# One more seven-product group for tile pairs 8 and 9, other planner costs, and a last product cut at column 256 in a fused attention and feed-forward kernel

## The chip, the cores and the metric

The kernel runs on one core of one Trainium2 chip. The metric is the device time of one execution in microseconds (us). A core has TensorE (PE in the profile; its weight loads are listed apart as PEld), VectorE (DVE), ScalarE (ACT), GpSimd (POOL), which here mostly issues loads, and SyncE (SP), which here issues stores. Each engine takes its instructions in the order in which they were written; engines wait for each other by semaphores.

## The reference

Softmax attention over 8 batches of 12 heads (448 tokens, head size 64) is followed by a feed-forward block over all 3584 tokens. Inputs and output are float32.

```python
def _attn_ref(q, k, v):
    scores = (1.0 / np.sqrt(q.shape[-1])) * np.matmul(q, k.transpose(0, 1, 3, 2))
    scores = scores - np.max(scores, axis=-1, keepdims=True)
    attn = np.exp(scores)
    attn = attn / (np.sum(attn, axis=-1, keepdims=True) + 1e-09)
    return np.matmul(attn, v)

def _moe_ref(x, w_in, w_out):          # w_in 768x2048, w_out 2048x768
    h = x @ w_in
    g = h * (1.0 / (1.0 + np.exp(-h)))
    return g @ w_out

# x = attention's output, heads side by side: 3584 x 768
```

## The kernel before

The matrices are kept in float16, sums in float32 in PSUM. Attention runs batch by batch, interleaved with the feed-forward products of batches that are done. The last four batches go through the first product, x @ w_in, two at a time (`queue_pair`, batches 4 and 5, then 6 and 7), by Winograd's form of Strassen's method: seven products in place of eight, paid for with additions on DVE. The tiles named f are theirs.

The second product, g @ w_out, is made for pairs of 128-token tiles, numbered `qd` from 0 to 13, again by seven products (`queue_quad`, `product`). Product m of a pair is eight matmuls, each with 128x128 weights (a slice of g or of a sum of such slices) and 384 columns of w_out (or of a difference of its quarters). The sums of g, called S_5, S_6, S_3 and 7, come from `combine_g` (line 918), each in two DVE instructions of 128x512. Products gather in PSUM tiles named p; ACT copies four of them into output tiles (`take_copy`, line 1006), DVE adds the rest (`take_sum`, line 1025) and SP stores them: four issues of 32 rows for each block of 128x384, except for the last batch. Output tiles are called ost (four buffers, taken in turn) or wide (for pairs 8, 10 and 11).

Some products of two neighbouring pairs use the same right-hand matrix. `FOLD` on line 255 lists those that are joined: the first two numbers are the pairs, the last tuple the products. Two such products, 16 matmuls of 384 columns, then form one 2x2 block product, which is made once more by seven products of a quarter of its size: four matmuls of 192 columns each (`queue_fold`, `fold_product`). Its left-hand sums are four DVE instructions of 128x512 (`fold_x`, line 1084, tiles named fold); its right-hand sums are made once for each m (`fold_w`, line 1062, tiles named right and T), for m = 4 and m = 2. The results gather in two PSUM tiles, n_P and n_Q, which five DVE instructions add to the two output blocks (`fold_read`, lines 1123, 1126 and 1135). From the third entry of `FOLD` on (`MID`) a group runs among the products of its second pair, has its PSUM tiles from the common banks, and holds some of the attention's old buffers for its left-hand sums: three of the four rq buffers and one of the two rk buffers for m = 2.

The order of all instructions is made by a planner inside the kernel. `Order.step` advances a model of the engines: each `Op` has an engine, a duration in us, the ops that it needs and a bias that ranks it among those that are ready. PE takes the first product in the queue `moe` that is ready by this model (`moe_ready`). For DVE and ACT a part of each duration counts as overlap with the next instruction (`OVERLAP`, 0.07 us on DVE). What comes out is a fixed order for each engine; the durations in the `Op` calls are not times of the chip, they only decide that order.

The last product of all is product 2 of pair 13. It is made in two pieces, each with its own PSUM tile (p and p_2r), its own DVE addition and its own stores (`take_end`, line 1012): the first piece is stored by SP alone, 128 rows, the second by SP and ACT, 64 rows each.

```python
FOLD = ((10, 11, (2, 4)), (12, 13, (4,)), *((7, 8, (4,)),))
...
for c in range(2):
    for f0 in range(0, HF, 1):
        queue(2, f0, f0 + 1, OH // 2 * c, OH // 2 * (c + 1))
```

Of the kernel before, what the change touches and what calls it, by code (L numbers as in the profile page):

```python
# [29 lines left out]
def mm(n):  # L30
    return n / 2400.0 + 0.0026
# [183 lines left out]
def kernel(  # L215
# [25 lines left out]
    OH = DM // 2  # L241
# [10 lines left out]
    FAR = (NT * B // 4 - 1,)  # L252
    BROAD = NT * B // 4 - 3
    WIDE = (NT * B // 4 - 6, NT * B // 4 - 4)
    FOLD = ((10, 11, (2, 4)), (12, 13, (4,)), *((7, 8, (4,)),))
    MID = 2
    AHEAD_OF = ((1, 4),)
    LEAD = 0
    TAIL = None
    folded = {(q, m) for a, b, ms in FOLD for q in (a, b) for m in ms}  # L260
    TWB, SXB = 40, 4
# [802 lines left out]
    def fold_x(g, m, i, at):  # L1064
        a, b = FOLD[g][:2]
        tag, n = at
# [19 lines left out]
    def fold_product(g, m, k):  # L1086
        a, b = FOLD[g][:2]
        x, y, bank, at, new = {
# [20 lines left out]
    def fold_read(g, m, k):  # L1109
        a, b = FOLD[g][:2]  # L1110
        i, j = {2: SUM[2], 4: OUT[4]}[m]
# [35 lines left out]
    od = Order(SHY)  # L1147
# [111 lines left out]
    def take_bank(name):  # L1259
        bank_of[name] = m_ring.take()  # L1260
# [357 lines left out]
    def plan_sums():  # L1618

        if not quads:  # L1620
            return
        qd, todo = quads[0]
        if len(todo) == 4:
            gates = {}
            for f in range(NFF):
                gates[f] = gates_at(2 * qd, f) + gates_at(2 * qd + 1, f)
                if None in gates[f]:
                    return
            gates_of[qd] = gates
        gates = gates_of[qd]  # L1630
        while todo and (todo[0] == 7 or sg_ring.can(1, od.now)):
            m = todo.pop(0)
            if m != 7:
                sg_ring.take()
            sg_op[(qd, m)] = []
            for f0 in (0, 4):
                deps = [x for f in range(f0, f0 + 4) for x in gates[f] + gates[f + HF]]
                if m != 5:
                    deps += sg_op[(qd, {6: 5, 7: 5, 3: 6}[m])]
                sg_op[(qd, m)].append(  # L1640
                    od.add(
                        Op(
                            "DVE",
                            0.40,
                            lambda m=m, f0=f0: combine_g(qd, m, f0, f0 + 4),
                            deps,
                            0,
                            then=lambda at, m=m: sum_read(qd, {6: 5, 3: 6}.get(m), at),
                        )
                    )  # L1650
                )
        if not todo:
            quads.pop(0)
# [3 lines left out]
    def plan_folds():  # L1657

        last = PAIRS[1]
        if "w" not in w2_op and last_pair and e_ring.can(1, od.now):  # L1660
            w2_op["w"] = True
            e_slot["spare"] = e_ring.take()
            for m in (4, 2):
                for i in (1, 2, 3, 4):
                    more = [w2_op[(m, i // 2)]] if i in (2, 4) else []
                    w2_op[(m, i)] = od.add(
                        Op("DVE", 0.57, lambda m=m, i=i: fold_w(m, i), last_pair + more, 1)
                    )
        if not folds or "w" not in w2_op:
            return  # L1670
        g, m, done = folds[0]
        made = [x for q in FOLD[g][:2] for f in range(HF, NFF) for x in gates_at(2 * q + m // 4, f)]
        n = len(x2_op) // 4
        if g < MID:
            if (last, HF - 1) not in pair_done:
                return
            made += [pair_done[(last, HF - 1)].get((i, j)) for i in range(2) for j in range(2)]
            if n > 2:
                made += [fold_done[n - 2].get(k) for k in (7, 2)]
        if None in made:  # L1680
            return
        held = ((rq_ring, 3), (rk_ring, 1)) if m == 2 else ((kt_ring, 2),)
        if g >= MID:
            if not all(r.can(k, od.now) for r, k in held):
                return
            for r, k in held:
                r.take(k)
            done["held"] = held
        folds.pop(0)
        homes = [("KT", 3)] * 3 + [("rk", NRK)] if n % 2 else [("rq", NRQ)] * 4  # L1690
        if g >= MID:
            homes = [("KT", 3)] * 2 + [("xT", NX3)] * 2 if m == 4 else [("rq", NRQ)] * 3 + [("rk", NRK)]
        for i in (1, 2, 3, 4):
            more = [x2_op[(g, m, i // 2)]] if i in (2, 4) else []
            x2_op[(g, m, i)] = od.add(
                Op("DVE", 0.43, lambda i=i: fold_x(g, m, i, homes[i - 1]), made + more, 1)
            )

    kept = []
# [96 lines left out]
    def queue_quad(qd):  # L1796
        quads.append((qd, [5, 6, 7, 3]))
        took = {}
# [14 lines left out]
        def queue(m, f0, f1, c0=0, c1=OH):  # L1813
            first = {6: (1,), 2: (1,), 7: (6, 5), 3: (5, 6) if qd == LAST else (5, 6, 7), 4: (7,)}.get(m, ())

            def run():
                strips = od.mode == "cols" and bool(qk_seq or av_seq)
                op = Op(
                    "PE",
                    (f1 - f0) * mm(c1 - c0),  # L1820
                    lambda: product(qd, m, f0, f1, strips, c0, c1),
                    tail=PE_OUT,
                )
                if BANK[m] == m and f0 == 0:
                    take_bank(f"p_{qd}_{m}" + "r" * (c0 > 0))
                for ring, need in rings:
                    ring.take(need)
                if m in (5, 6, 3) and f1 == HF:
                    op.then = lambda at: sum_read(qd, m, at)
                od.on_pe(op, "cols" if strips else "full", (f1 - f0) * (4 if strips else 1))  # L1830
                if f1 < HF or c1 < OH:
                    begun[m] = (HF if c0 else 0) + f1
                if f1 < HF:
                    return
                if c1 - c0 < OH:
                    fn = lambda: take_end(half_t[c0][:, 0 : c1 - c0], c0, c1)
                    od.add(Op("DVE", 0.33, fn, [op, took[1]], -4))
                    return
                pr_op[(qd, m)] = op
                read(m, [op] + [took[x] for x in {2: (1,), 7: (5,), 3: (6,)}.get(m, ())])  # L1840
                if m == 7 and (qd, 4) in folded:
                    if qd in ahead:
                        def then(at):
                            leave_bank(f"p_{qd}_1")(at)
                            home.give(at + STORE)

                        od.add(
                            Op(
                                "DVE",
                                OH / 960.0 + 0.13,  # L1850
                                lambda: take_last(qd),
                                [op, took[7], ahead[qd]],
                                -4,
                                then=then,
                            )
                        )
                    else:
                        read(4, [op, took[7]])

            def deps():  # L1860
                if f0 or c0:
                    return [] if begun.get(m) == (HF if c0 else 0) + f0 else [None]
                made = list(w_op.get(m, [None]))
                hard = {6: (1,), 7: (6,), 3: (5,), 4: (7,)}.get(m, ())
                made += [took.get(x) if x in hard else (took.get(x), 9.0) for x in first]
                if m in (1, 2, 4):
                    t = 2 * qd + m // 4
                    i = int(m != 1)
                    for f in range(HF):
                        made += [(y, f * mm(OH)) for y in gates_at(t, f + HF * i)]  # L1870
                    return made + ld_wout
                x = sg_op.get((qd, m), [None, None])
                return made + [x[0], (x[1], 4 * mm(OH))]

            rings = ((home, 1),) if f0 == 0 and (m in OUT or m == 7 and (qd, 4) in folded and qd not in ahead) else ()
            moe.append((deps, int(BANK[m] == m and f0 == 0), run, rings))


# [18 lines left out]
        if qd == LAST and TAIL:  # L1897
            ends.pop()()
        elif qd == LAST:
            for c in range(2):  # L1900
                for f0 in range(0, HF, 1):
                    queue(2, f0, f0 + 1, OH // 2 * c, OH // 2 * (c + 1))

    def after_x(n):

# [56 lines left out]
    qk_seq, av_seq = [], []  # L1962
# [287 lines left out]
    while True:  # L2250
# [45 lines left out]
        m = m_ring.when(1)  # L2296
# [43 lines left out]
```

## Time and profile before

| | us |
|---|---|
| median of 3 runs | 378.93 (378.29 to 379.14) |
| the profiled execution, device time | 378.17 |
| its span on the core | 376.4 |
| PE busy | 370.2 |
| DVE busy | 287.5 |
| ACT busy | 255.6 |

The span runs from the first to the last instruction of the core. Busy time is the time in which an engine had at least one instruction in work. A matmul in the records lasts longer than its distance to the next one, since matmuls are pipelined: 384 columns are shown with 326 ns and follow each other every 163, 192 columns are shown with 246 ns and follow every 82. DVE and ACT instructions overlap their neighbours in the records too, by some 0.08 and 0.1 us. In the timeline a line is one instruction, or several alike in a row ("x8"); the name before the arrow is what is written, the names behind it what is read, and a bracket tells how long the engine had been idle and what ended that.

### The profile page before, as it was taken

To read this page: it belongs to the slowest core of one execution; us is meant where nothing else is said; L and a number is where in the kernel's file an instruction comes from. 1 tells how busy PE (TensorE), PEld (TensorE's weight loads), DVE (VectorE), ACT (ScalarE), POOL (GpSimd) and SP (SyncE) were. 2 spreads that over 40 slices of the span, in tenths; PEclk is the share of its full clock that TensorE was granted. 3 is DMA by queue.
4 is the path that set the end of the run, shared out by engine and by line. 5 is a ranking of instruction groups with operands and counts; after the bars stand their busy time and mean duration, and the time that the engine had idled before them with its cause. 6 is when DMAs were issued, how large, how long until landed. Compare 5 with 4: busy or idle time off the path is not lost.

```text
span 376.4 us, 9978 instructions
## 1 busy us (share of the span) xinstructions
PE 370.2 (98%) x4030; PEld 188.0 (50%) x4030; DVE 287.5 (76%) x597; ACT 255.6 (68%) x401; POOL 85.0 (23%) x155
## 2 busy tenths in 40 slices
PE   7999999999999999999999999999999999999996
PEld 3365445444444444444444454545556655556764
DVE  3668858999995969995969998899379725449853
ACT  4988873896878787877788777658872238883130
POOL 6653337424016326006423200000000000000000
PEclk9999999999999999999999999999999999999999
DMA  7999999919049849147954411210002240001334
GB/s 113 198 208 209 207 200 181 205 21 132 16 96 153 154 51 123 27 94 108 176 91 67 57 46 44 55 32 0 0 3 53 74 108 20 0 1 34 84 96 126
DMA packets 35966, 34.47 MB, mean 92 GB/s; under 512 B 11856, under 2 KB 35152, under 8 KB 35920
## 3 DMA queue, kind: packets, MB, share of 16 engines
q0 software_dynamic: 25312, 22.82, 40.9%
q1 hardware_dynamic: 10064, 10.38, 10.1%
q10 hardware_dynamic: 544, 0.64, 0.5%
q8 instruction: 31, 0.51, 0.5%
q14 instruction: 15, 0.12, 0.1%
HBM read 45.61 MB, written 11.01 MB: 150 GB/s over the span
## 4 chain that ended last, share of the span: by engine, by line
PE 95%; ACT 3%; DMA 1%; DVE 0%; issue 0%; POOLq 0%
PE p L685 29%; PE h L685 21%; PE f L685 16%; PE s L448 11%; PE a L570 8%; PE o L685 3%; ACT E L504 2%; PE a L556 2%; PE a L603 2%; PE n_Q L685 1%; PE n_P L685 1%; DMA rk<-in_k_dram 1%; ACT T L493 1%; PE z L685 0%; PE p_2r L685 0%
## 5 line engine op out<-in xcount | busy, mean ns | idle before, releaser
L504 ACT ACTIVATE E<-s 128x896 f16<-128x896 f32 x164 | 141.9, 921 | 24.5 <-PE s L448 24.5
L685 PE MATMUL h<-xT,w_in_t 128*32 128x448 f16 (+2 forms) x762 | 83.5, 348 | 0.0
L685 PEld LDWEIGHTS <-w_in_t 128*128 128x128 f16 (+1 forms) x909 | 54.6, 97 | 50.0 <-issue 8.0
L354 POOL DMA_DIRECT2D V<-in_v_dram x88 | 48.5, 560 | 51.2 <-PE a L570 29.2
L685 PEld LDWEIGHTS <-G 128*128 128x128 f16 (+1 forms) x668 | 41.9, 97 | 28.0 <-issue 5.2
L717 ACT ACTIVATE th<-h 128x448 f16<-128x448 f32 x67 | 36.6, 546 | 24.2 <-PE h L685 20.7
L685 PE MATMUL p<-w_out_t,G 128*128 128x384 f16 (+2 forms) x326 | 51.8, 324 | 0.0
L448 PE MATMUL s<-rq,KT 32*128 32x448 f16 (+3 forms) x728 | 44.9, 347 | 1.4 <-DVE rq L412 0.9
L685 PEld LDWEIGHTS <-S 128*128 128x128 f16 (+1 forms) x321 | 29.5, 98 | 22.3 <-issue 3.4
L761 DVE SCALAR_TENSOR_TENSOR G<-th,h 128x448 f16<-128x448 f16 (+1 forms) x64 | 35.7, 573 | 4.8 <-ACT th L717 4.3
L685 PE MATMUL p<-D,S 128*128 128x384 f16 (+1 forms) x217 | 39.0, 326 | 0.0
L1006 ACT COPY ost<-p 128x384 f32<-128x384 f32 x38 | 18.2, 480 | 24.6 <-PE p L685 16.2
L570 PE MATMUL a<-E,V 128*32 128x448 f16 (+1 forms) x640 | 32.7, 356 | 0.0
L1025 DVE TENSOR_TENSOR ost<-p,ost 128x384 f32<-128x384 f32 x29 | 16.0, 553 | 18.4 <-ACT ost L1006 9.6
L673 DVE SCALAR_TENSOR_TENSOR xT<-a,rdn 128x448 f16<-128x448 f32 x46 | 27.0, 619 | 3.0 <-PE a L570 2.4
L334 POOL DMA_DIRECT2D rq<-in_q_dram x25 | 13.9, 559 | 67.3 <-PE s L448 57.9
L448 PEld LDWEIGHTS <-KT 32*128 32x128 f16 (+1 forms) x824 | 12.3, 96 | 31.5 <-issue 29.8
L517 DVE TENSOR_TENSOR T<-T,E 128x1792 f16<-128x1792 f16 x21 | 22.8, 1086 | 4.7 <-ACT E L504 4.7
L888 DVE TENSOR_TENSOR p<-f,p 128x448 f32<-128x448 f32 x15 | 9.4, 624 | 22.2 <-PE f L685 12.3
L517 DVE TENSOR_TENSOR T<-E,E 128x1792 f16<-128x1792 f16 x21 | 22.8, 1084 | 4.0 <-ACT E L504 4.0
L685 PE MATMUL f<-sx,tw 128*128 128x448 f16 x102 | 23.4, 352 | 0.0
L570 PEld LDWEIGHTS <-V 128*32 128x32 f16 (+1 forms) x640 | 13.5, 95 | 18.0 <-issue 10.1
(134 smaller groups left out, 464.5 us busy)
## 6 DMA issues: line engine op xcount, KB each, us to landing
out_dram<-ost SPq DMA_DIRECT2D x147, 48.0 KB, 1.8
rk<-in_k_dram POOLq DMA_DIRECT2D x24, 224.0 KB, 5.4
rq<-in_q_dram POOLq DMA_DIRECT2D x23, 224.0 KB, 5.7
w_out_t<-in_moe_w_out_dram POOLq DMA_DIRECT2D x4, 768.0 KB, 13.5
V<-in_v_dram POOLq DMA_DIRECT2D x42, 64.0 KB, 4.0
out_dram<-wide SPq DMA_DIRECT2D x48, 48.0 KB, 1.6
V<-in_v_dram POOLq DMA_DIRECT2D x42, 48.0 KB, 4.4
w_in_t<-in_moe_w_in_dram POOLq DMA_DIRECT2D x6, 256.0 KB, 8.7
```

Source lines behind the costliest of these rows:

```text
L334: nc.gpsimd.dma_start(out=rawq[n][:, cols], in_=group_of(q, b, hg)[:, cols])
L354: nc.gpsimd.dma_start(out=VT[b][32 * x : 32 * (x + 1), hs, at : at + count, :], in_=v[b, hs].rearrange("h (i g) d -> i h g d", g=TPP)[:, : ...
L448: nc.tensor.matmul(out=pS[p0 : p0 + 32 * (x1 - x0), h % 2, at : at + q1 - q0], lhsT=KT[(b, hg)][32 * h : 32 * (h + 1), key_rows(b, hg, c, ...
L504: nc.scalar.activation(out=E[(n, w)][:, 2 * y : 2 * y + 2, :], in_=pS_t[(n, w, y)][:, :, 0:S], func=AF.Exp, scale=attn_scale,)
L517: nc.vector.tensor_tensor(out=T[n], in0=T[n] if step else E[(n, 0)], in1=E[(n, step + 1)], op=ALU.add,)
L570: nc.tensor.matmul(out=a[32 * h : 32 * (h + 1), 0:S], lhsT=VT[b][k0:k1, HG * hg + h, place(b, hg, c), part - 1 :: 2], rhs=e[k0:k1, h], sta ...
L673: nc.vector.scalar_tensor_tensor(out=x3(b, cc)[:, cc % 3, 32 * g0 : 32 * g1], in0=acc[(n, part)][:, 0:nq], scalar=0.5, in1=rdn_t[n].rearra ...
L685: nc.tensor.matmul(out=out[i : i + cut], lhsT=w[:, i : i + cut], rhs=x, start=start, stop=stop, skip_group_check=True,)
L717: nc.scalar.activation(out=th, in_=h_t[(b, f, t0)][:, 0:n], func=AF.Tanh)
L761: nc.vector.scalar_tensor_tensor(out=dst[:, f, at + lo : at + hi], in0=th_t[(b, f, t0)][:, lo - t0 : hi - t0], scalar=1.0, in1=h_t[(b, f, ...
L1006: nc.scalar.copy(out=ost(qd, *OUT[m]), in_=bank(qd, BANK[m]))
L1025: nc.vector.tensor_tensor(out=t, in0=bank(qd, BANK[m]), in1=t, op=ALU.add)
```

## The change

Three things. Product 2 of pairs 8 and 9 is joined and made by seven quarter products. The planner's durations of three kinds of DVE instruction are other ones: sums of g 0.35 in place of 0.40 once attention's scores are all issued (`qk_seq` is empty), left-hand sums of groups 0.36 in place of 0.43, and the additions of the last product by their columns. The last product is divided into 256 and 128 columns in place of twice 192.

```diff
-    FOLD = ((10, 11, (2, 4)), (12, 13, (4,)), *((7, 8, (4,)),))
+    FOLD = ((10, 11, (2, 4)), (12, 13, (4,)), *((7, 8, (4,)), (8, 9, (2,))))
...
                         Op(
                             "DVE",
-                            0.40,
+                            0.40 if qk_seq else 0.35,
                             lambda m=m, f0=f0: combine_g(qd, m, f0, f0 + 4),
...
-                Op("DVE", 0.43, lambda i=i: fold_x(g, m, i, homes[i - 1]), made + more, 1)
+                Op("DVE", 0.36, lambda i=i: fold_x(g, m, i, homes[i - 1]), made + more, 1)
...
                     fn = lambda: take_end(half_t[c0][:, 0 : c1 - c0], c0, c1)
-                    od.add(Op("DVE", 0.33, fn, [op, took[1]], -4))
+                    od.add(Op("DVE", (c1 - c0) / 960.0 + 0.13, fn, [op, took[1]], -4))
...
-            for c in range(2):
+            for c0, c1 in ((0, 256), (256, OH)):
                 for f0 in range(0, HF, 1):
-                    queue(2, f0, f0 + 1, OH // 2 * c, OH // 2 * (c + 1))
+                    queue(2, f0, f0 + 1, c0, c1)
```

The new group is the fourth entry of `FOLD`, so it is a group of the second kind: it runs among the products of pair 9 and takes its banks from the common ones. Its reads go to the blocks of product 2, a wide tile of pair 8 and an ost tile of pair 9. SP's stores of that block of pair 8 come after those of pair 9.

## The prediction

> **What bounds the kernel now.** I read the page first: busy shares, granted clock, the chain that ended last.
>
> ```profile
> span 376.4 us, 9978 instructions
> PE 370.2 (98%) x4030; PEld 188.0 (50%) x4030; DVE 287.5 (76%) x597; ACT 255.6 (68%) x401; POOL 85.0 (23%) x155
> ...
> PE 95%; ACT 3%; DMA 1%; DVE 0%; issue 0%; POOLq 0%
> ```
>
> TensorE (PE) is the chain. So a matmul taken out is a gain, and any wait put into PE's queue is a loss in full, because no later gap takes it back. The second view is the busy time by stretch (columns PE, PEld, DVE, ACT, POOL, clock, DMA share, GB/s), since the 76% of VectorE (DVE) is an average.
>
> ```profile
> 280.00:300.00 20.00, 20.00 (x139) 12.96 (x138) 18.74 (x48) 4.84 (x11) 0.00 (x0) 1.00 0.22 55
> 300.00:310.00 10.00, 10.00 (x61) 5.76 (x60) 1.68 (x3) 3.78 (x8) 0.00 (x0) 1.00 0.42 106
> ```
>
> From 280 to 300 us, where pairs 7, 8 and 9 are prepared and multiplied, DVE is busy 18.74 of 20 us; from 300 to 310 it is nearly idle. PE never stops, but DVE is a close second in the first stretch. How close is in the timeline (start, length, engine, line, operation), the third view:
>
> ```profile
> 286.60 0.75 DVE L918 TENSOR_TENSOR S<-G,S 128x512 f16<-128x512 f16 x2
> ...
> 287.72 1.46 PE L685 MATMUL p<-w_out_t,S 128*128 128x384 f16 x8
> ...
> 294.49 0.56 DVE L1025 TENSOR_TENSOR wide<-p,wide 128x384 f32<-128x384 f32 x1
> ...
> 295.08 0.48 ACT L1006 COPY wide<-p 128x384 f32<-128x384 f32 x1 [2.78 <-DVE wide L1025]
> ...
> 296.01 0.49 PE L685 MATMUL n_Q<-right,G 128*128 128x192 f16 x4
> ...
> 297.36 0.55 DVE L1135 TENSOR_TENSOR wide<-n_Q,wide 128x384 f32<-128x384 f32 x1
> ...
> 297.98 0.49 PE L685 MATMUL n_Q<-D,fold 128*128 128x192 f16 x4
> ```
>
> These are three handovers from DVE to PE. The third sum S_3 of pair 7 is half ready at 287.01 and used at 287.72: about 0.6 us spare. The add at 294.49 ends at 295.05, lets ScalarE (ACT) copy until 295.56, and PE wants the result at 296.01: 0.4 spare. The add at 297.36 ends at 297.91 and PE starts at 297.98: nothing spare. The end of the kernel is the fourth view:
>
> ```profile
> 371.27 0.82 PE L685 MATMUL p<-w_out_t,G 128*128 128x192 f16 x8
> 371.54 0.56 DVE L1025 TENSOR_TENSOR ost<-p,ost 128x384 f32<-128x384 f32 x1 [0.81 <-PE p L685]
> 371.93 0.82 PE L685 MATMUL p_2r<-w_out_t,G 128*128 128x192 f16 x8
> 372.13 0.36 DVE L1012 TENSOR_TENSOR ost<-p,ost 128x192 f32<-128x192 f32 x1
> 372.55 1.09 SPq L1016 DMA_DIRECT2D out_dram<-ost  x2
> 372.79 0.36 DVE L1012 TENSOR_TENSOR ost<-p_2r,ost 128x192 f32<-128x192 f32 x1 [0.30 <-PE p_2r L685]
> 373.23 0.49 ACTq L1016 DMA_DIRECT2D out_dram<-ost  x1
> ```
>
> **Steps that I use.** Each is the distance from start to start of neighbours in this timeline. Matmul of 384 columns 0.1625 us, of 192 columns 0.0825 (297.98 minus 297.82 gives the first; four take 0.33). DVE: 128x512 f16 0.335, 128x768 f16 0.47, add of 384 columns 0.475, of 192 columns 0.265, the 128x1344 one 0.81. From the end of a DVE instruction to a PE matmul that waits for it: 0.07.
>
> **Part 1, matmuls.** Product 2 of pairs 8 and 9 goes: 16 x 0.1625 = 2.60. Seven products of four 192-column matmuls come: 28 x 0.0825 = 2.31. PE gains 0.29 us. The right-hand sums for product 2 are made today for pairs 10 and 11, so nothing is added there.
>
> **Part 2, DVE.** Added: four left-hand sums, 4 x 0.335 = 1.34; reads of 2 x 0.265 and 3 x 0.475 = 1.96. Removed: two adds, 0.95. Net 2.35 us. The reads fall after 301 us, where DVE is idle; the four sums fall between 281 and 291, where it is full, while only one removed add (0.475) comes from there.
>
> **Part 3, the planner's costs.** A 128x512 sum is now planned at 0.35 (left-hand sums 0.36), of which the planner takes off 0.07 for overlap: 0.28 against the 0.335 measured; before it was 0.33 (and 0.36). The planner writes PE's order by these numbers, so that order now expects DVE 0.055 earlier per such instruction. It also moves sums: first halves of later sums stand ahead of adds that free a bank.
>
> **Part 4, the walk.** I walk the queues of the changed kernel in its built order with the steps above. Until 280.30 nothing differs.
> - S_3 of pair 7: three 128x512 instructions of the new group (sums 1, 3 and 2) now stand ahead of it, and nothing that stood there has left: 286.60 + 3 x 0.335 = 287.60, first half ready at 288.02, weights loaded and used at about 288.13. PE has one more matmul ahead of it than before: 287.72 + 0.16 = 287.88. Wait 0.25. Everything on PE is behind it.
> - The add of pair 8's first block: from 287.60 DVE goes on without a gap (13 of 128x512, two adds of 384, one of 192, two of 768 and the 1344 one: 7.32) and starts it at 294.92, 0.43 later than before. It ends at 295.48, the ACT copy at 295.99, and PE could start at 296.04. PE has lost the eight matmuls of product 2 as cover and arrives after 42 x 0.1625 + 8 x 0.0825 = 7.49 us, at 295.62. Wait 0.42.
> - The read of product 5 of the group of pairs 7 and 8: both halves of S_3 of pair 9 (0.67) are now ahead of it; it starts 2.89 after the add before, at 297.81, and frees PE at 298.43, and PE, with twelve matmuls of 192 and six of 384 (1.97) from 296.04, arrives at 298.00. Wait 0.43.
> - Pair 9: product 7 needs the ACT copy of product 6 (0.20 drain, 0.48 copy, 0.05), and only two quarter products (0.66) stand between now, not a full product 2 (1.30). Wait 0.07.
> - After 340 us the order is nearly the same work with DVE's sums a little earlier in it. One add of pair 11, 0.33 spare before, now has two half sums (0.67) ahead of it; by the walk it costs 0.14, others 0.04. With the 0.07 this is 0.25.
> Sum of waits: 0.25 + 0.42 + 0.43 + 0.25 = 1.35. Bounds: with DVE's step 0.01 shorter throughout (the 0.75 rows allow 0.33) about 0.7 is left, with 0.01 longer 2.2. I keep 1.35, since the same walk over the old order meets the recorded starts of DVE and PE to 0.1 us up to the end.
>
> **Part 5, buffers and stores.** The new group holds three of four q buffers and one of two k buffers until about 307.8, so product 1 of the next f, which stood between pair 9's products at 304.33 as filler, goes behind them; the group's own products take that place, at no cost beyond the waits above. The stores of pair 8's first block move behind those of pair 9 on SP's queue (four issues of 0.465 each); SP ends about 1 us later, near 312. The next owner of these buffers comes after 340, which hides it.
>
> **Part 6, the end.** The last 16 matmuls have the same columns. On the line through the 384 and 192 rows, (0.1625 - 0.0825)/192 per column, 256 columns take 0.109 and 128 take 0.056: 8 x 0.109 + 8 x 0.056 = 1.32, as 16 x 0.0825 = 1.32. The last add shrinks by 64 columns, from 0.36 to about 0.29, and does not wait for the first (which ends 0.02 before it can start): -0.06. The first store's issue on SP (0.36) begins 0.28 later (0.21 of matmuls, 0.07 of the add), so SP's half of the last store starts about 0.12 later than now; the records show that half landing 0.30 before ACT's half, so ACT's half, now 0.06 earlier, ends the kernel. Bounds for 128 columns: 0.056 on the line, 0.0825 if the weight load set the pace of the 192 row; I take the line, because the 192 and 384 rows lie on one line with the 448 row (0.19) and show no floor.
>
> The Trainium skill, "TensorE: Matmul & The Clock Gate", section "Back-to-back issue gap", speaks against this piece: it gives some 81 ns as the sustained gap at 128 columns and 56 ns for an isolated one. By the sustained figure the last piece would cost 8 x 25 ns = 0.20 us more, an estimate from that page. Its sustained figure for 512 columns, 131 ns, does not agree with this trace, where 448 columns take 190 ns; at 128 columns no run here shows it.
>
> **Sum.** -0.29 + 1.35 - 0.06 = +1.00: span 376.4 to 377.4, and with the 1.77 around it (378.17 - 376.40) 379.2 for the profiled execution. That one is 0.76 below the median of the runs, 378.93, so the median comes to 379.9.
>
> **Rivals.**
> - Hidden after all: DVE's four sums fit and PE waits nowhere. For it: 1.26 us of DVE idle time between 280 and 300. Against: the idle time lies late, and the new sums come early. -0.29 - 0.06 = -0.35: 378.6, not slower. It decides if S_3 of pair 7 is ready by 287.8.
> - DVE becomes the bound of the stretch: each wait delays the matmuls that DVE itself reads next, and the waits compound to the 2.2 above. For it: the third handover has nothing spare. Against: DVE catches up in the idle stretch from 300. +1.85: 380.8.
> - The weight load sets the pace at 128 columns: 8 x (0.0825 - 0.056) = 0.21 on top of the forecast: 380.1. For it: the 192 row is the shortest full-width one here. Against: its place on the line. The page's rule named above is this mechanism.
>
> **Chances.** Forecast 0.57 (its own range 379.5 to 380.4), weight pace 0.16, DVE bound 0.13, hidden 0.14. A difference under 0.2%, 0.76 us, can't be told from none. Slower by more: 0.82 of the forecast, 0.85 of the weight pace, all of the DVE bound: 0.73. Faster by more: a quarter of "hidden": 0.04. Within: 0.23. The range is 379.1 (forecast with the shorter DVE step, 378.93 - 0.35 + 0.7 = 379.28, and 0.2 for the spread of the runs) to 380.8.
>
> **What would show it.** Matmuls of 128x192 in the rows of n_P and n_Q up by 28. PE idle in the records at about 288, 296 and 298 us (a wait shows less its modelled drain of 0.16: some 0.1, 0.24 and 0.27), released by DVE, ACT and DVE. The add from p_2r at about 0.29. Wrong: no idle there, or the product p_2r with starts 0.08 apart.

## The result, and the profile after

The changed kernel takes 379.26 us (median of 22 runs, 378.79 to 380.45), the kernel before, run beside it, 378.93 (22 runs). The ratio of the runs is 1.0019 [1.0011, 1.0026], that is +0.72 us [0.42, 0.99]; the two medians alone differ by 0.33 us, the two means by 0.59. The profiled execution took 379.63 us with a span of 377.9.

The page first, the same three lines as were read before:

```profile
span 377.9 us, 10004 instructions
PE 371.3 (98%) x4042; PEld 188.9 (50%) x4042; DVE 289.3 (77%) x604; ACT 255.5 (68%) x401; POOL 85.0 (22%) x155
...
PE 92%; DMA 3%; DVE 3%; POOL 1%; issue 1%; POOLq 0%
```

PE has 12 matmuls more (28 in, 16 out), and DVE now stands in the chain of waits with 3%: PE is stopped by it somewhere. The busy time by stretch says where:

```profile
280.00:300.00 20.00, 19.50 (x133) 12.19 (x130) 19.52 (x51) 5.55 (x12) 0.00 (x0) 1.00 0.17 43
300.00:310.00 10.00, 10.00 (x76) 6.79 (x75) 3.87 (x8) 2.35 (x6) 0.00 (x0) 1.00 0.39 99
```

DVE went from 18.74 to 19.52 of 20 us, and PE, which was at 20.00, is idle for 0.50 there. The timeline shows the three handovers of the prediction:

```profile
281.91 1.46 PE L685 MATMUL p<-D,S 128*128 128x384 f16 x8
...
288.29 0.75 DVE L918 TENSOR_TENSOR S<-G,S 128x512 f16<-128x512 f16 x2
...
288.41 0.33 PE L685 MATMUL p<-D,S 128*128 128x384 f16 x1
...
288.76 1.47 PE L685 MATMUL p<-w_out_t,S 128*128 128x384 f16 x8
...
294.44 0.85 DVE L817 TENSOR_TENSOR sx<-xT,sx 128x1344 f16<-128x1344 f16 x1
...
295.55 0.55 DVE L1025 TENSOR_TENSOR wide<-p,wide 128x384 f32<-128x384 f32 x1
...
296.13 0.48 ACT L1006 COPY wide<-p 128x384 f32<-128x384 f32 x1 [2.94 <-DVE wide L1025]
...
296.66 0.49 PE L685 MATMUL n_Q<-right,G 128*128 128x192 f16 x4 [0.24 <-ACT wide L1006]
...
298.42 0.55 DVE L1135 TENSOR_TENSOR wide<-n_Q,wide 128x384 f32<-128x384 f32 x1
...
299.02 0.49 PE L685 MATMUL n_Q<-D,fold 128*128 128x192 f16 x4 [0.23 <-DVE wide L1135]
```

At 288.41 a matmul of 384 columns starts, and the next one, which reads S_3, only 0.35 later instead of 0.163: a wait of 0.19. At 296.66 and 299.02 the brackets show 0.24 and 0.23 of idle time; the modelled drain of the matmul before, 0.16, belongs to the wait too, so these are 0.41 and 0.40. All are counted below as the distance between starts, less the usual one.

**A yardstick.** Spans of single executions can't be compared directly here: this one is already 0.69 us later than the one before at 280 us, where both kernels have run the same instructions. The offset arises in the first 40 us and then stays; other executions stand between -0.3 and +0.7 at the same place. So I use the *stretch*: from the first matmul of pair 7's product 5 (281.91 above, 281.22 before) to the end of the span. It is 95.95 us now and 95.14 before: +0.81. A second profiled execution of the changed kernel gives 95.96. In the kernel before it starts here:

```profile
281.22 1.46 PE L685 MATMUL p<-D,S 128*128 128x384 f16 x8
```

The end of the kernel:

```profile
372.89 1.04 PE L685 MATMUL p<-w_out_t,G 128*128 128x256 f16 x8
...
373.76 0.61 PE L685 MATMUL p_2r<-w_out_t,G 128*128 128x128 f16 x8
373.96 0.42 DVE L1012 TENSOR_TENSOR ost<-p,ost 128x256 f32<-128x256 f32 x1 [0.25 <-PE p L685]
374.41 0.29 DVE L1012 TENSOR_TENSOR ost<-p_2r,ost 128x128 f32<-128x128 f32 x1
374.45 0.92 SPq L1016 DMA_DIRECT2D out_dram<-ost  x2
374.78 0.51 ACTq L1016 DMA_DIRECT2D out_dram<-ost  x1
```

From the first matmul of the last product to the end of the span it is 4.97 us; before it was 5.09. So the cut gains 0.12. About half of it lies ahead of the last landing, which comes 3.99 after the product's start instead of 4.05. The rest lies behind it: SP waits for its stores in a fixed order, which takes 0.06 for each that has already landed, and before, one more of them came after the store that landed last.

**Where the time went.** All distances over the usual one, in the trace of after; the times are those of the last matmul before the wait:

| wait of PE | forecast | measured |
|---|---|---|
| S_3 of pair 7, 288.4 | 0.25 | 0.19 |
| ACT copy of pair 8's block, 296.1 | 0.42 | 0.41 |
| read of product 5 of group (7, 8), 298.5 | 0.43 | 0.40 |
| pair 9's product 7, 302.7 | 0.07 | 0.07 |
| pair 11, 359.2 | 0.14 | 0.12 |
| others (306.9, 353.8, 357.6) | 0.04 | 0.08 |
| sum | 1.35 | 1.27 |

The kernel before has one such wait, 0.03 at 352.3, so the net is 1.24. With the matmuls at -0.29 and the end at -0.12 the sum is +0.83, against +0.81 in the stretch.

### The profile page after: what moved, and what is told of

Same layout as the page of the kernel before. It is cut to its first block, busy times and chain, and to the rows that moved or that the text cites. A ratio compares the mean times of both kernels' runs of the same rounds, so it can differ in the third digit from the quotient of the medians.

```text
span 377.9 us, 10004 instructions
## 1 busy us (share of the span) xinstructions
PE 371.3 (98%) x4042; PEld 188.9 (50%) x4042; DVE 289.3 (77%) x604; ACT 255.5 (68%) x401; POOL 85.0 (22%) x155
## 4 chain that ended last, share of the span: by engine, by line
PE 92%; DMA 3%; DVE 3%; POOL 1%; issue 1%; POOLq 0%
PE p L685 27%; PE h L685 21%; PE f L685 16%; PE s L448 10%; PE a L570 8%; DMA rk<-in_k_dram 3%; PE o L685 3%; PE a L603 2%; PE n_Q L685 2%; PE a L556 2%; PE n_P L685 1%; DVE S L918 1%; POOL V L354 1%; DVE KT L397 0%; PE z L685 0%
## 5 line engine op out<-in xcount | busy, mean ns | idle before, releaser
L685 PE MATMUL p<-w_out_t,G 128*128 128x384 f16 (+2 forms) x310 | 49.1, 325 | 0.0
```

Of the source, the lines that this page charges most:

```text
L685: nc.tensor.matmul(out=out[i : i + cut], lhsT=w[:, i : i + cut], rhs=x, start=start, stop=stop, skip_group_check=True,)
```

## The experiments

**Theory.** DVE's added work and the planner's shorter durations together make PE late: the order expects DVE before it can be there. **Rivals:** the new group alone does it, by DVE's work; the durations alone do it; the cut at 256 costs or gives more than its 0.06. Measured by the stretch of one profiled execution each, the kernels come out as follows ("waits" as counted above; "made of" = waits - 0.03 before, -0.29 where the group is in, -0.11 for the cut):

| kernel | waits | made of | stretch, against 95.14 |
|---|---|---|---|
| changed | 1.27 | +0.84 | 95.95, +0.81 |
| e1: group and cut, old durations | 0.40 | -0.03 | 95.08, -0.06 |
| e2: durations and cut, no group | 0.33 | +0.19 | 95.32, +0.18 |
| e3: cut alone | 0.04 | -0.10 | 95.03, -0.11 |
| e4: group and cut, measured durations | 0.13 | -0.30 | 94.82, -0.32 |
| e5: changed, half of the new left sums | 0.92 | +0.49 | 95.63, +0.49 |
| e6: group and cut, sums of g 0.35 only | 0.88 | +0.45 | 95.55, +0.41 |
| e7: group and cut, left sums 0.36 only | 0.41 | -0.02 | 95.09, -0.05 |

The 0.11 is e3's own result, so e3 tests nothing in its row; the others are made up of waits to within 0.04 us. Where a kernel was profiled twice (the changed one, and e4), its two stretches agree to 0.01 us.

### One part at a time: e1, e2, e3

e1 keeps the group and the cut, and takes the durations back:

```diff
-                            0.40 if qk_seq else 0.35,
+                            0.40,
...
-                Op("DVE", 0.36, lambda i=i: fold_x(g, m, i, homes[i - 1]), made + more, 1)
+                Op("DVE", 0.43, lambda i=i: fold_x(g, m, i, homes[i - 1]), made + more, 1)
```

> The change with the planner's durations of the sums set back (0.40 and 0.43); the new group and the cut at 256 stay. Yardstick: the stretch from the first matmul of pair 7's product 5 to the end of the span, 95.14 us before and 95.95 with the change; the same instructions stand ahead of it in both. Theory (the planner's short durations bring PE too early to DVE's sums): PE waits once, about 0.28, near 292, and 0.1 near 301 and 305; waits 0.4 in all in place of 1.27; stretch 95.1; time 0.0 to 0.2 under before. Rival (the four sums are too much for DVE in that stretch, however they are planned): waits of 0.8 or more, stretch 95.5 or more.

e2 keeps the durations and the cut, and takes the group out:

```diff
-    FOLD = ((10, 11, (2, 4)), (12, 13, (4,)), *((7, 8, (4,)), (8, 9, (2,))))
+    FOLD = ((10, 11, (2, 4)), (12, 13, (4,)), *((7, 8, (4,)),))
```

> The change without the new group: only the planner's shorter durations and the cut at 256. Theory: DVE has nothing more to do, yet PE comes too early: waits of 0.15 near 298, 0.14 near 358 and 0.06 elsewhere; stretch 95.14 + 0.32 - 0.12 = 95.3. Rival (the group's sums alone make the waits): no waits beyond the 0.03 of before; stretch 95.0, as with the cut alone.

e3 is the kernel before with the cut at 256 alone (`for c0, c1 in ((0, 256), (256, OH)):`).

> The cut at 256 alone. The profile of the changed kernel shows 56 ns between matmuls of 128 columns and an end 0.12 nearer to the last product's start than before. Theory: stretch 95.14 - 0.12 = 95.0, no wait added. Rival (the larger first store on SP delays the last one, and the shorter end of that one profile was chance): 95.1 to 95.25.

Measured: e1 378.17 us, ratio 0.9995 [0.9985, 1.0005]; e2 378.56, 1.0002 [0.9992, 1.0012]; e3 378.47, 0.9998 [0.9988, 1.0008] (12 runs each; the kernel before, 35 runs, 378.43). None of the three can be told from the kernel before by its runs. The stretch can tell them: against e3, the group alone costs 0.05, the durations alone 0.29, both together 0.92. So neither rival accounts for the loss alone: together the two parts cost far more than the 0.34 of both taken singly. The group puts 2.35 us of work on DVE, and with the old durations the order finds room for most of it.

Not all. In e1 the order is again one that DVE can't keep, at another place:

```profile
291.55 0.55 DVE L1025 TENSOR_TENSOR ost<-p,ost 128x384 f32<-128x384 f32 x1
291.56 0.49 PE L685 MATMUL n_P<-D,G 128*128 128x192 f16 x4
...
292.16 1.14 PE L685 MATMUL p<-w_out_t,G 128*128 128x384 f16 x6
```

The four matmuls take 0.33, to 291.89; the next product starts at 292.16, 0.06 after the add that ends at 292.10. That is 0.27 of wait on DVE, nearly as much as the saved matmuls bring. Less the 0.07 that the planner takes off, the old durations are 0.33 and 0.36: the first is close to the measured step of 0.335, the second, that of the left sums, is too long. With shorter left sums (e7 and e4 below) this wait is gone.

### Less work on DVE: e5

From the changed kernel, the new group's left sums are made half as wide, in the same order:

```diff
-        nc.vector.tensor_tensor(out=x2_t[(g, m, i)], in0=x, in1=y, op=op)
+        w = 2 if g == 3 else 4
+        nc.vector.tensor_tensor(out=x2_t[(g, m, i)][:, 0:w], in0=x[:, 0:w], in1=y[:, 0:w], op=op)
...
-            times(t, x[:, f, :], y[:, f, :], new and f == 0, f == 3, False)
+            fx = f % 2 if g == 3 and k in (6, 7, 5, 3) else f
+            times(t, x[:, fx, :], y[:, f, :], new and f == 0, f == 3, False)
```

> The changed kernel with the planner's durations and so every engine's order as they are, but the four left-hand sums of the new group made over half their columns (128x256 in place of 128x512); its products read the half that is made twice, so the output blocks of product 2 of pairs 8 and 9 are left wrong. DVE is shorter by some 0.13 us at each of the four. Theory (PE waits for the end of DVE's queue): the wait at S_3 of pair 7 (0.19) goes, the one at the ACT copy of pair 8 (0.41) falls by some 0.15, the one at the read of product 5 (0.40) stays, since its DVE instructions are queued behind PE's own product; stretch about 95.95 - 0.33 = 95.6. Rival (the waits come from the banks or the stores of the new group, not from DVE's time): all three stay, stretch 95.9.

One execution, 378.75 us beside 378.96 for the kernel before; it leaves out half of each new left sum, so the two output blocks are wrong. Its timeline:

```profile
287.49 0.75 DVE L918 TENSOR_TENSOR S<-G,S 128x512 f16<-128x512 f16 x2
...
288.01 1.46 PE L685 MATMUL p<-w_out_t,S 128*128 128x384 f16 x8
...
294.62 0.56 DVE L1025 TENSOR_TENSOR wide<-p,wide 128x384 f32<-128x384 f32 x1
...
295.21 0.48 ACT L1006 COPY wide<-p 128x384 f32<-128x384 f32 x1 [2.78 <-DVE wide L1025]
...
295.74 0.49 PE L685 MATMUL n_Q<-right,G 128*128 128x192 f16 x4
...
297.48 0.56 DVE L1137 TENSOR_TENSOR wide<-n_Q,wide 128x384 f32<-128x384 f32 x1
...
298.10 0.49 PE L685 MATMUL n_Q<-D,fold 128*128 128x192 f16 x4 [0.23 <-DVE wide L1137]
```

With the order unchanged and DVE relieved, the wait for S_3 is gone and that for the ACT copy falls from 0.41 to 0.24: DVE's work is the cause of these. The third stays at 0.40, although DVE is earlier everywhere. It is a distance within the order: DVE's read comes 2.86 us after the add at 294.62, as it comes 2.87 after the add at 295.55 in the changed kernel, because the same instructions stand between them. Less work ahead of both does not touch it; it takes less work between the two, or another order.

### Which duration, and the right one: e6, e7, e4

e6 is e1 with the sums of g at `0.40 if qk_seq else 0.35`; e7 is e1 with the left sums at `0.36`; e4 plans both at the measured step plus the 0.07 that the planner takes off:

```diff
-                            0.40,
+                            0.405,
...
-                Op("DVE", 0.43, lambda i=i: fold_x(g, m, i, homes[i - 1]), made + more, 1)
+                Op("DVE", 0.405, lambda i=i: fold_x(g, m, i, homes[i - 1]), made + more, 1)
```

> The change with the shorter planned duration for the sums of g alone (0.35); the left-hand sums are planned at 0.43 as before. Theory: most of the loss comes from this number, for the sums of g are many: waits of 0.2 near 296, 0.4 and 0.16 near 298, 0.1 later; stretch about 95.6. Rival (the number for the new group's own sums decides): waits of 0.4 in all, stretch 95.1, as with the old durations.

> The change with the shorter planned duration for the left-hand sums alone (0.36); the sums of g are planned at 0.40 as before. Theory: waits of 0.1 and 0.15 near 297 to 298 and 0.2 elsewhere, 0.45 in all; stretch about 95.15. Rival (this number decides): waits of 1.0 or more, stretch 95.7 or more.

> The change with the planner's durations of the sums set to what the profile shows: 0.405 each, which is the 0.335 between neighbours and the 0.07 of overlap that the planner takes off. Theory: the group fits: waits of 0.07 near 301 and 0.06 elsewhere, 0.13 in all; stretch 95.14 - 0.29 + 0.10 - 0.12 = 94.8, 0.3 under before and 0.3 under the run with the old durations. Rival (DVE has no room for the sums): stretch 95.5 or more, as the changed kernel.

e6 ran in 379.65 us and e7 in 378.04 (one run each, beside 378.96). In the stretch, e6 is 0.47 over e1, e7 within 0.01 of it. With both short, as in the changed kernel, it is 0.87. So the short duration of the sums of g costs about half of the loss by itself; that of the left sums costs nothing alone, and the other 0.40 on top of the first. There are many sums of g and few left sums, which may be why the first weighs more; no run tests that. e4 ran in 378.13, ratio 0.9993 [0.998, 1.0005]; in the stretch it is the shortest of all, 0.21 below e3. Of the 0.29 that the removed matmuls can bring, 0.08 is given back, nearly all in two small waits of pair 9 (0.07 and 0.02).

### The two orders again, beside each other: r_changed, r_measured_costs

> The changed kernel once more, beside the next one on the same chip. Theory: the same waits and a stretch of 95.95 in its profile; the time 0.1 to 0.25% over before, 0.3% over the next kernel.

> The change with the planned durations at 0.405, once more, for a direct comparison with the changed kernel. Theory: stretch 94.8; the time 0.3% under the changed kernel and 0.0 to 0.15% under before. Rival (the gain in the stretch is lost ahead of or behind it): no difference to the changed kernel beyond 0.1%.

The changed kernel: 379.50 us, ratio 1.0023 [1.0009, 1.0037]. The one with measured durations: 377.91, ratio 0.9986 [0.9974, 0.9997] (12 runs each; the kernel before, 23 runs, 378.64). So the group, planned rightly, clearly beats the changed kernel, and the kernel before by little: 0.5 us [0.1, 1.0] here, while e4's runs, on another chip, could not tell the two apart. In the stretch, 0.11 of its gain of 0.32 is the cut's and 0.21 the group's. The busy time by stretch and the timeline of the latter:

```profile
280.00:300.00 20.00, 20.00 (x138) 12.96 (x137) 19.55 (x51) 5.38 (x12) 0.00 (x0) 1.00 0.20 50
```

```profile
287.90 0.75 DVE L918 TENSOR_TENSOR S<-G,S 128x512 f16<-128x512 f16 x2
...
288.76 1.46 PE L685 MATMUL p<-w_out_t,S 128*128 128x384 f16 x8
...
294.16 0.55 DVE L1025 TENSOR_TENSOR wide<-p,wide 128x384 f32<-128x384 f32 x1
...
294.74 0.48 ACT L1006 COPY wide<-p 128x384 f32<-128x384 f32 x1 [2.38 <-DVE wide L1025]
...
295.60 0.49 PE L685 MATMUL n_Q<-right,G 128*128 128x192 f16 x4
...
296.86 0.56 DVE L1135 TENSOR_TENSOR wide<-n_Q,wide 128x384 f32<-128x384 f32 x1
...
297.56 0.49 PE L685 MATMUL n_Q<-D,fold 128*128 128x192 f16 x4
...
298.46 0.85 DVE L817 TENSOR_TENSOR sx<-xT,sx 128x1344 f16<-128x1344 f16 x1
```

DVE is as busy as in the changed kernel (19.55 and 19.52 of 20 us), and PE doesn't stop. The copy ends at 295.22 and PE comes at 295.60; the read ends at 297.42 and PE comes at 297.56. What moved is the order: the 1344-column add, 0.81 us, starts at 298.46, behind the three handovers. In the changed kernel it stood ahead of two of them, at 294.44. It is the longest piece that moved, but not the only one: the two halves of pair 9's S_3, which stood ahead of the read, now come behind it. And its place alone does not decide: in e7 the add also starts ahead of both handovers, at 293.75, and the waits are 0.41 in all.

### Durations shorter still: e9

Both durations at 0.31 (`0.40 if qk_seq else 0.31`, and `0.31`), the rest as in the changed kernel.

> The changed kernel with both planned durations lowered once more, to 0.31 (a step of 0.24 in the planner against 0.335 on the chip). Theory: the waits grow with the error of the plan: 0.2 near 284, 0.7 near 295, 0.7 near 297 and 0.5 later, 2.1 in all in place of 1.27; stretch 96.7. Rival (the order has saturated and the waits come from the group's own chain): 1.3 in all, stretch 95.9.

One execution. The waits sum to 2.07, close to the 2.1 expected. The two large ones, 0.75 and 0.69, stand at another read, that of an n_P bank, and at the ACT copy:

```profile
294.55 0.49 PE L685 MATMUL n_P<-T,fold 128*128 128x192 f16 x4 [0.58 <-DVE ost L1123]
...
296.86 0.49 PE L685 MATMUL n_Q<-right,G 128*128 128x192 f16 x4 [0.53 <-ACT wide L1006]
```

At the read of product 5, the third handover of the changed kernel, PE does not wait here. The time does not fit: 381.44 us, and a stretch of 98.56 where 96.7 was expected. Up to the last matmul the stretch is 0.81 longer than that of the changed kernel (93.06 and 92.25), which is the waits; the other 1.8 lies behind the last matmul, where it takes 5.50 instead of 3.70. The rows of its DMA issues from 374 us on (size, then us from issue to landing):

```profile
q8 instruction: 1, 0.02, 1.0%
...
out_dram<-ost SPq DMA_DIRECT2D x1, 128.0 KB, 3.9
out_dram<-ost ACTq DMA_DIRECT2D x1, 32.0 KB, 3.7
out_dram<-ost SPq DMA_DIRECT2D x1, 32.0 KB, 3.8
```

In the changed kernel the same three take this long, and no packet of the instruction queue is among them:

```profile
out_dram<-ost SPq DMA_DIRECT2D x1, 128.0 KB, 1.7
...
out_dram<-ost ACTq DMA_DIRECT2D x1, 32.0 KB, 1.8
out_dram<-ost SPq DMA_DIRECT2D x1, 32.0 KB, 2.0
```

So the last stores landed some 2 us later, beside one packet of 16 KB that took 0.93 us. The packets and landing signals in the trace tell more. Each of these stores gives 16 signals. Fifteen of them come as in the changed kernel, by 376.19, 376.61 and 376.89; the last one comes at 378.34, 378.51 and 378.69. The 16 KB packet runs from 376.22 to 377.15, and the packets of the late part, 19 of them, move one after another from 377.13 to 378.06. So one sixteenth of each store was held up behind that packet. Why the first eight of those 19 packets took 0.05 to 0.14 us each, where 0.04 to 0.05 is usual, is not shown. The same 16 KB packet is in the traces of e1, e5, e6 and e8 too, but there it starts 1.8 to 3.0 us after the last packet of a store and holds up nothing. So the 1.8 us come from when the packet ran, and they are not waits of PE; what sets that time, and whether e9 meets it in every execution, stays open with one execution.

### Is there a floor under short matmuls? e8

The last product is cut at 320 of 384 columns (`((0, 320), (320, OH))`), so that its last eight matmuls have 64.

> The changed kernel with the last product cut at 320, so that the second piece has 64 columns, to see how close matmuls with 128x128 weights can follow each other. On the line through 384, 192 and 128 columns (162, 82 and 56 ns) 64 columns would take 29 ns. Theory A (only the columns count): 29 to 30 ns, the eight of p_2r start within 0.21 us. Theory B (a weight load of 128x128 sets a floor between 29 and 56): 40 to 56 ns, the last product 0.1 to 0.2 longer. The first addition over 320 columns takes about 0.49 and now ends after the second piece, so the end comes 0.1 later at least: from the last product's start to the end of the span 5.05 or more, against 4.97 in the changed kernel.

```profile
371.88 1.25 PE L685 MATMUL p<-w_out_t,G 128*128 128x320 f16 x8
...
372.97 0.40 PE L685 MATMUL p_2r<-w_out_t,G 128*128 128x64 f16 x8
373.17 0.49 DVE L1012 TENSOR_TENSOR ost<-p,ost 128x320 f32<-128x320 f32 x1 [0.46 <-PE p L685]
373.58 0.21 DVE L1012 TENSOR_TENSOR ost<-p_2r,ost 128x64 f32<-128x64 f32 x1
```

Eight matmuls of 320 columns take 372.97 - 371.88 = 1.09, 136 ns each; those of 64 columns follow every 28 to 30 ns. There is no floor down to there, although each weight load is shown with 98 ns. From the last product's start to the end of the span it is 5.03, a little under the 5.05 expected as the least, and 0.06 more than with 256: the first piece's add, whose store SP must issue first, starts 1.29 after the product's start (373.17 - 371.88) instead of 1.07. The run took 378.69 us.

## Why the prediction was right, and where it was off

The direction, the mechanism and the three main places held. The size was too large: +1.00 forecast, +0.81 in the stretch, +0.72 [0.42, 0.99] by the ratio of the runs, +0.33 between the medians. For the median itself 379.9 was forecast and 379.26 measured. That is below the range that the forecast gave for itself, 379.5 to 380.4; it is inside the whole range, 379.1 to 380.8, because the lower end allowed for a shorter DVE step and for the spread of the runs.

- **Matmuls, -0.29.** Held: PE's rows show 12 more instructions, and the sums of all the experiments close with it.
- **S_3 of pair 7.** DVE starts it at 288.29, which less the offset of 0.69 is 287.60, as walked. The wait is 0.19 and not 0.25: the walk gave 0.11 from the end of the first half to PE, and the trace shows about 0.05.
- **ACT copy and read.** The adds start at 294.86 and 297.73 less the offset; walked were 294.92 and 297.81. Waits 0.41 and 0.40, forecast 0.42 and 0.43.
- **The rest, 0.25.** Measured 0.27, of which 0.03 was there before.
- **The end, -0.06.** This step failed in its mechanism. I let ACT's half of the last store end the kernel, as in the kernel before. It now lands at 376.61 and SP's at 376.88: SP issues two stores one after the other (0.92 for both), and its second one is now the late one. ACT's half came forward by more than the 0.06 of the shorter add: it is issued 1.89 after the product's start instead of 1.96, and lands 1.8 after that instead of 2.1, with 32 KB in place of 48. SP's is issued 2.01 after the product's start instead of 1.91, about as forecast, but takes 2.0 to land instead of 1.8; the forecast had kept the old times to landing for both halves. The last landing is 0.06 nearer to the product's start, but by another half than forecast, so that this size agrees is luck. With the 0.06 behind the landing the gain is 0.12.
- **Buffers and stores.** Free, as forecast, but mis-sized: SP's stores of this stretch end at 314.1 instead of 311.3, which is 2.2 later after the offset where about 1 was expected. SP's next store comes after 345, and PE waits nowhere for it.
- **Planner's costs.** Named as one part of the cause without a price of their own. e1 and e2 give it: against the cut alone, the group without them costs 0.05, they without the group 0.29, both together 0.92.

Of the rivals, *hidden after all* fell for this kernel: S_3 was not there at 287.8. But it is what e4 does; it needs the right order, not less work. *DVE becomes the bound* fell by its size, 1.27 of waits against 2.2; e9 shows that the waits do grow to 2.07 when the plan is further off. *Weight pace* fell: p_2r's matmuls start 56 ns apart at 128 columns, and 28 to 30 ns apart at 64 in e8. The 81 ns that the Trainium skill gives in "TensorE: Matmul & The Clock Gate", section "Back-to-back issue gap", as the sustained gap at 128 columns does not agree with the 56 ns of this trace; its isolated figure of 56 ns does.

The forecast was too high for two reasons that add: the waits came out 0.11 smaller net, and the end gained 0.06 more than forecast.

## What to carry to other kernels

Work taken from the bounding engine and given to a second one that is nearly full can be paid for by the order more than by the amount: here the same instructions, the cut's 0.11 included, cost +0.81 us or gained 0.32, depending on the durations that the planner was told. The amount still counts: e5, with less DVE work in the same order, took 0.32 off the stretch. When an order is written from planned durations, set them to the distances that the trace shows (plus whatever the planner takes off), and then look at each handover for the work that stands ahead of it. Judge changes of this size by a stretch of the trace with identical work ahead of it, since single executions differ by as much before they reach it.

## What the runs showed of the hardware

- Matmuls with a new full weight load each follow one another every 163, 136, 109, 82, 56 and 28 to 30 ns at 384, 320, 256, 192, 128 and 64 columns: a straight line of some 0.42 ns for each column and 2 ns of constant (granted clock 1.00). The loads themselves are shown with 98 ns (e8) and do not set the pace.
- After 280 us of identical instructions, executions stood -0.3 to +0.7 us from that of the kernel before; where it was followed, in the changed kernel, the +0.7 arose in the first 40 us.
- In e9 one sixteenth of each of the last three stores landed some 2 us late, behind a 16 KB packet of the instruction queue (376.22 to 377.15); in e1, e5, e6 and e8 the same packet came after the stores and cost nothing.
